# Gate and value products of chunks 1 to 5 by half-size Winograd products in PSUM lanes, the residual by accumulating transfers, and a new instruction order

## The chip, the cores and the metric

One core of a Trainium2 chip runs the whole program in one launch. The metric is device microseconds of one execution, less is better. Besides the timed runs there is one execution taken by the hardware profiler; its span goes from the first to the last instruction of the core. The engines are PE (TensorE, matmuls), ACT (ScalarE), DVE (VectorE), POOL (GpSimd) and SP (SyncE, which only issues transfers here).

## The reference

Inputs are q, k and v of shape (4 batches, 8 heads, 768 tokens, 64). Three heads (0, 2, 6) are causal; the five others see only the first 4 keys and the last 64.

```python
scores = q @ k.transpose(0, 1, 3, 2) / sqrt(64)          # masked, softmax, then @ v
x      = attention, heads side by side                   # 3072 tokens x 512
g      = x @ w_gate                                      # 512 x 1536
val    = x @ w_val                                       # 512 x 1536
ffn    = (0.5 * g * (1 + erf(g / sqrt(2))) * val) @ w_out    # 1536 x 512
out    = x + sigmoid(x @ w_res) * ffn                    # f32
```

## The kernel before

**Tiling.** The 3072 tokens are cut into six chunks of 512 (four tiles of 128): chunk 0 and 3 are the first four tiles of batches 0 and 2, chunks 1 and 4 are two tiles of one batch and two of the next, chunks 2 and 5 four tiles of batches 1 and 3. A chunk goes through attention (by pairs of heads: scores on PE, exp on ACT, masks on DVE, values on PE, normalizing on DVE into `xtok` in f32 and `x` in f16, transposes into `xT`), then gate and value, then the output product. Chunks overlap: while gate and value of one chunk run, the output product of the chunk before ends, and the next chunk's scores follow.

**Gate and value** (`gate_value`). There are 12 column tiles f of 128 for gate and for value. Each is four matmuls of 512 columns (the tokens; the weights are the stationary operand) into a PSUM bank. ACT makes the gelu (L1166), DVE multiplies with the value bank into `hT` (L1168). Chunk 0 starts in halves of 256 tokens (L1140, L1143).

**Output** (`output_fast`, all but half of chunk 0). The product h @ w_out is already done by Winograd's form of Strassen's scheme: tokens, inner dimension and columns are each halved, and seven products of half size replace eight. `sums` forms S1 to S4 from h (L1187), `weight_sums` T1 to T4 from w_out (L1204); two PSUM banks take the products, and partial results go out and are added by ACT and DVE (L1251, L1252, L1257). Then DVE multiplies by 1 + tanh (L1281) and adds x (L1286), and SP stores 256 KB per tile (L1292).

**Loads.** POOL issues the loads of q, k, v and of the weights, which convert f32 to f16 on the way (L577). Chunks 0 and 1 transpose q and k on PE (L709), the later ones by transposing transfers of SP (L754) into `qkt`; a further transfer copies one pair of heads of it to the lower partitions (`q`, L762).

**Order.** Every operation is a task with a duration, dependences, buffers and a priority. `Graph.schedule` plays the program through with fixed costs (`c_mm`, `c_act`, `c_dve`, and a cost per transfer) and writes a fixed sequence for every engine; `HINTS` replaces the priorities of single tasks by tuned numbers. Buffers come from pools, and a task waits for the last users of the slot that it gets. On the chip each engine then runs its sequence in order and waits on semaphores. In the first 20 us PE runs filler matmuls on a blank tile (L1333) where nothing else is ready; they end with the first gate product. From chunk 2 on many matmuls run as two halves of 64 columns (`mm`, L516 whole, L517 halves).

Of the kernel before, what the change touches and what calls it, by code (L numbers as in the profile page):

```python
# [43 lines left out]


HINTS = (
    "3:-58.9 11:-130.04 428:854.14 430:718.61 444:2782.08 457:-821.9 460:407.45 490:4205.68 521:1522.06 "
    "591:-818.43 610:-36.63 612:486.89 613:-2965.25 619:1544.03 621:-44.07 643:467.87 644:-881 646:4.3 656:119.6 "
    "664:25.04 673:629.62 675:-109.25 695:-2674.26 696:-1856.67 703:-881.5 706:-108.75 707:714.39 708:1939.7 "
    "711:270.02 712:497.18 716:476.22 720:652.56 738:638.32 743:520.23 744:3053.24 749:514.3 750:1799.28 "  # L50
    "751:2383.53 756:521.28 762:1469.72 764:4344.87 767:2237.74 787:-603.93 815:5053.25 817:2978.67 821:1231.87 "
    "824:1484.86 836:2402.62 837:798.1 841:706.04 848:-288.52 849:2997.07 876:2751.74 906:2555.54 913:1516.93 "
    "918:2437.99 919:1519.88 924:1537.25 931:1510.23 936:2384.32 949:2443.79 955:2089.28 967:2846.74 995:-227.38 "
    "1001:29.83 1002:3171.86 1003:3180.29 1004:1146.58 1007:2686.58 1012:1781.89 1040:-803.29 1043:1907.45 "
    "1045:1028.83 1046:667.33 1050:3229.28 1051:1536.45 1053:3573.03 1056:-1823.77 1084:4090.27 1110:2454.97 "
    "1111:2597.62 1117:2808.38 1123:2507.5 1128:2481.58 1129:2529.63 1134:2508.5 1146:2434.73 1152:2779.33 "
    "1153:3034.61 1158:3861.94 1165:2795.06 1171:3076.63 1176:2997.8 1185:5989.69 1188:2243.92 1189:2528.84 "
    "1192:2789.39 1193:2537.45 1194:3836.22 1208:3021.15 1215:6294.68 1263:3219.13 1268:5037.38 1283:4420.5 "
    "1308:4756.92 1311:3513.6 1317:3517.03 1321:3052.3 1329:5930.49 1330:3507.5 1335:3508.5 1336:3519.22 "
    "1341:4624.14 1345:3444.6 1353:3516.64 1354:3538.83 1357:2761.66 1365:3787.63 1366:5173.04 1372:5102.72 "  # L60
    "1386:5438.32 1392:4014.31 1393:4933.66 1418:5146.68 1430:4133.91 1441:5428.8 1452:5127.54 1457:2188.42 "
    "1462:4595.33 1464:5711.23 1467:9389.54 1468:4425.54 ~1471:550.69 1476:5611.77 1499:4504.13 1513:6742.83 "
    "1516:5340.27 1522:4510.5 1523:4585.63 1526:3632.38 1534:4503.02 1539:4253.34 1550:4463.64 1565:7711.51 "
    "1570:4506.5 1571:5085.34 1580:2427.42 1594:2466.44 1610:9272.71 1625:3048.93 1627:6036.71 1629:6167.81 "
    "1631:5064.12 1644:6476.5 1662:4125.72 1671:5044.95 1672:7314.6 1676:4967.2 1683:6427.71 1692:9540.12 "
    "1711:7387.16 1757:5137.62 1784:5507.1 1797:5469.41 1803:7562.23 1817:7773.49 1818:7478.69 1823:7672.83 "
    "1834:7419.08 1836:10250.4 1849:7490.55 "
# [123 lines left out]
VS_DMA = 0  # L191
LAT = {"pe": 0.20, "act": 0.10, "dve": 0.08, "pool": 0.12, "sp": 0.1}


class Graph:
# [205 lines left out]
    def emit(self):  # L401
# [31 lines left out]
        with nc.Block() as blk:  # L433
# [17 lines left out]
            @blk.sync  # L451
            def _(e):
                run("sp", e)
                for t in finals:
                    e.wait_ge(t.sem, 16)
# [6 lines left out]
def c_act(n):  # L462
    return 0.19 + n * 0.000834


def c_dve(n, rate=1.0, psum=True):
    return (0.125 if psum else 0.065) + n * 0.00104 / rate
# [6 lines left out]
def build_kernel(nc, q, k, v, w_gate, w_val, w_out, w_res, out):  # L474
# [17 lines left out]
    P_vs = Pool(many("vs", 2, [128, NT - 1, NHEAD, DHEAD + 1], FP16))  # L492
    P_vk = Pool(many("vk", 2, [128, 8, DHEAD + 1], FP16))
    P_qkt = Pool(many("qkt", 2, [128, 2, NPAIR, SEQ], FP16))
# [9 lines left out]
    P_hs = Pool(many("hS", 1, [128, 3, NF // 2, 2, 128], FP16))  # L504
    wt = sb("wt", [128, 4, NF // 2, 256], FP16)
    P_ga = Pool(many("gact", 4, [128, 512], FP16))
    P_sr = Pool(many("srs", 3, [128, 512], FP32))
# [5 lines left out]
    def mm(e, o, lhsT, rhs, **k):  # L513
# [8 lines left out]
        "gv": (4, one(6, 7, 5, 4, 3, 2)), "gv0": (4, one(6, 7, 5, 4)), "gvh": (4, one(7, 6, 4, 5)), "out": (2, one(6, 7)), "fin": (4, one(6, 7, 1, 0)), "warm": (1, one(7, 5)),  # L522
# [81 lines left out]
    def batch(b):  # L604
        if b not in batches:
            B_ = B()
            B_.v, B_.vs, B_.vk, B_.qkt = Buf(P_v), Buf(P_vs), Buf(P_vk), Buf(P_qkt)
            B_.vtok, B_.vstok, B_.qtok, B_.ktok = {}, {}, {}, {}

            B_.q6, B_.q6tok = None, {}  # L610
            batches[b] = B_
        return batches[b]

    def values(b, a, z, base, each, on_engines=False):
# [23 lines left out]
        if on_engines:  # L638
            ts = []
            for lo, hi, pr in ((1, 2, -75),) + (() if VS_DMA else ((2, 4, 130),)):  # L640
                for dst, src, off in ((0, 64, 1), (64, 0, 0)):
                    def vs(on, dst=dst, src=src, off=off, lo=lo, hi=hi):
                        def fn(e):
                            o = at(BB.vs)[dst:dst + 64, lo - 1:hi - 1, :, :].rearrange("p i h d -> p (i h d)")
                            i_ = at(BB.v)[src:src + 64, lo - off:hi - off, :, :].rearrange("p i h d -> p (i h d)")
                            return e.activation(out=o, in_=i_, func=AF.Copy) if on == "act" else e.tensor_copy(out=o, in_=i_)
                        return fn
                    n_ = (hi - lo) * 520
# [9 lines left out]
        for lo in cuts:  # L658
            hi = lo + 1 if each else z
            ts = []  # L660
            for dst, src, off in ((0, 64, 1), (64, 0, 0)):
                ts.append(G.add("sp", 1.2, (lambda lo=lo, hi=hi, dst=dst, src=src, off=off: lambda e: e.dma_start(
                    at(BB.vs)[dst:dst + 64, lo - 1:hi - 1, :, :].rearrange("p i h d -> p (i h d)"),
                    at(BB.v)[src:src + 64, lo - off:hi - off, :, :].rearrange("p i h d -> p (i h d)")))(),
# [7 lines left out]
    def loads_rows(c, si, b, a, z):  # L672
# [17 lines left out]
        for gi, (h0, h1) in enumerate(groups):  # L690
# [41 lines left out]
    def loads_natural(c, si, b, a, z):  # L732
# [33 lines left out]
        for i in range(a, z):  # L766
            BB.q6tok[0, i] = BB.q6tok[1, i] = t
# [677 lines left out]
```

The softmax here doesn't subtract the row's maximum and nothing guards it: scores larger than these inputs give would overflow.

## Time and profile before

| | |
|---|---|
| timed runs, us | 267.08, 266.18, 265.86; median 266.18 |
| span of the profiled execution, us | 263.7 |
| time of the profiled execution outside its span | not recorded |
| PE busy, us | 257.7 (98% of the span) |
| DVE, ACT, POOL busy, us | 181.6, 147.2, 89.3 |
| granted PE clock | 1.000 |
| first gate product starts, us | 19.7 |
| last matmul ends, us | 257.4 |
| transfers, MB (share of 16 engines) | POOL's queue 14.69 (67.5%), SP's queue 14.07 (28.0%) |

In the profile a row of a group has line, engine, operation, the tiles written and read, shapes and count, then busy time and the mean of one in ns, then idle time of the engine before it and who ended it. A row of the timeline has start, length, engine, line, operation and count. Lengths of matmuls overlap, so the rate is read from the starts.

### The profile page before, as it was taken

The numbers are of one execution on the slowest core, as the hardware profiler recorded it, in microseconds if no ns is written. First come the engines' busy times: TensorE is split into PE (matmuls) and PEld (weight loads), VectorE is DVE, ScalarE is ACT, GpSimd is POOL, SyncE is SP. The second block draws the span as 40 slices with busy tenths as digits, with TensorE's granted clock in tenths as the row PEclk, the third lists the DMA queues.
The fourth block names the chain that finished last, engine by engine and source line by source line (L and its number), as shares of the span: only waits on it lengthen the run. The fifth ranks groups of instructions, "written<-read, shape, count | busy, mean of one in ns | idle before, by whom it ended". The sixth has DMA issues, their size and how long they took to land.

```text
span 263.7 us, 7495 instructions
## 1 busy us (share of the span) xinstructions
PE 257.7 (98%) x3226; PEld 164.0 (62%) x3226; DVE 181.6 (69%) x378; ACT 147.2 (56%) x237; POOL 89.3 (34%) x127
## 2 busy tenths in 40 slices
PE   7999999999999999999999999999999999999993
PEld 6777655468444668544567444589655588655692
DVE  2698437798447888557898366888557689837655
ACT  2785467974244987423787242967243888233430
POOL 8999979506109973975000000000000000000003
PEclk9999999999999999999999999999999999999999
DMA  6999999999999999999996110004200004200003
GB/s 83 174 204 206 188 175 231 175 153 204 134 200 148 165 137 177 171 179 176 174 156 150 42 40 0 2 26 101 82 2 0 2 2 122 82 2 0 2 35 127
DMA packets 96513, 29.22 MB, mean 111 GB/s; under 512 B 84449, under 2 KB 93025, under 8 KB 96481
## 3 DMA queue, kind: packets, MB, share of 16 engines
q0 software_dynamic: 70320, 14.69, 67.5%
q1 hardware_dynamic: 26160, 14.07, 28.0%
q8 instruction: 25, 0.41, 0.7%
q14 instruction: 8, 0.06, 0.1%
HBM read 29.36 MB, written 6.29 MB: 135 GB/s over the span
## 4 chain that ended last, share of the span: by engine, by line
PE 95%; DMA 2%; DVE 1%; issue 0%; POOLq 0%
PE ps L516 50%; PE ps L517 32%; PE ps L893 5%; PE ps L1333 2%; PE ps L1017 2%; PE ps L709 2%; DMA qks<-in_q_dram 2%; PE ps L1106 2%; PE ps L984 1%; DVE otile L1281 1%; DVE otile L1286 1%; DVE otile L1257 0%; POOLq L1427 0%
## 5 line engine op out<-in xcount | busy, mean ns | idle before, releaser
L1166 ACT ACTIVATE gact<-ps 128x512 f16<-128x512 f32 x68 | 40.2, 597 | 73.5 <-PE ps L516 43.7
L1168 DVE SCALAR_TENSOR_TENSOR hT<-gact,ps 128x512 f16<-128x512 f16 x68 | 46.1, 686 | 48.0 <-PE ps L516 23.1
L516 PE MATMUL ps<-xT,wg 128*128 128x512 f16 (+1 forms) x208 | 50.0, 363 | 0.0
L516 PE MATMUL ps<-xT,wv 128*128 128x512 f16 (+1 forms) x202 | 49.0, 362 | 0.0
L1286 POOL TENSOR_TENSOR otile<-otile,xtok 128x256 f32<-128x256 f32 x3 | 2.4, 801 | 136.2 <-DVE otile L1281 136.2
L577 POOL DMA_DIRECT2D qks<-in_k_dram x36 | 28.0, 810 | 17.3 <-DMA qkt<-qks 13.9
L516 PEld LDWEIGHTS ps<-xT,wg 128*128 128x128 f16 x208 | 20.1, 98 | 20.0 <-DVE otile L1257 0.3
L516 PEld LDWEIGHTS ps<-xT,wv 128*128 128x128 f16 x202 | 19.4, 98 | 20.0 <-DVE hT L1168 0.5
L577 POOL DMA_DIRECT2D qks<-in_q_dram x36 | 28.4, 828 | 2.2 <-issue 1.4
L517 PE MATMUL ps<-xT,wv 128*64 128x512 f16 x204 | 28.3, 380 | 0.0
L577 POOL DMA_DIRECT2D va<-in_v_dram x24 | 21.3, 920 | 15.1 <-PE ps L516 15.1
L517 PE MATMUL ps<-xT,wg 128*64 128x512 f16 x192 | 26.3, 379 | 0.0
L909 ACT ACTIVATE ea<-ps 128x1024 f16<-128x1024 f32 (+2 forms) x24 | 21.1, 915 | 1.7 <-PE ps L893 1.6
L1257 DVE TENSOR_TENSOR otile<-otile,ps 128x256 f32<-128x256 f32 x33 | 13.6, 417 | 7.1 <-PE ps L517 4.7
L1226 ACT ACTIVATE srs<-ps 128x512 f32<-128x512 f32 x22 | 13.1, 595 | 9.1 <-PE ps L517 6.7
L517 PEld LDWEIGHTS ps<-xT,wv 128*64 128x64 f16 x204 | 11.5, 110 | 9.8 <-DVE hT L1168 0.3
L1084 DVE TENSOR_TENSOR xtok<-ps,rcp 128x512 f32<-128x512 f32 (+1 forms) x28 | 16.8, 606 | 0.2
L517 PEld LDWEIGHTS ps<-xT,wg 128*64 128x64 f16 x192 | 11.1, 110 | 9.0
L893 PE MATMUL ps<-qkt 64*128 64x64 f16 (+4 forms) x391 | 16.4, 213 | 0.0
L893 PEld LDWEIGHTS ps<-qkt 64*128 64x128 f16 x391 | 9.8, 94 | 8.0 <-issue 4.2
L516 PE MATMUL ps<-wo,hT 128*128 128x256 f16 (+1 forms) x84 | 14.4, 304 | 0.0
L1286 DVE TENSOR_TENSOR otile<-otile,xtok 128x512 f32<-128x512 f32 (+1 forms) x21 | 14.3, 691 | 0.2
(109 smaller groups left out, 437.4 us busy)
## 6 DMA issues: line engine op xcount, KB each, us to landing
out_dram<-otile SPq DMA_DIRECT2D x22, 256.0 KB, 2.4
va<-in_v_dram POOLq DMA_DIRECT2D x24, 128.0 KB, 17.6
qks<-in_k_dram POOLq DMA_DIRECT2D x32, 64.0 KB, 12.6
qks<-in_q_dram POOLq DMA_DIRECT2D x32, 64.0 KB, 13.0
wg<-in_moe_w_gate_dram POOLq DMA_DIRECT2D x3, 512.0 KB, 10.2
wv<-in_moe_w_val_dram POOLq DMA_DIRECT2D x3, 512.0 KB, 12.1
wo<-in_moe_w_out_dram POOLq DMA_DIRECT2D x4, 384.0 KB, 22.8
vs<-va SPq DMA_DIRECT2D x4, 260.0 KB, 7.9
```

The costliest lines, as they stand in the source:

```text
L516: return e.matmul(o, lhsT=lhsT, rhs=rhs, **k)
L517: return [e.matmul(o[h:h + 64], lhsT=lhsT[:, h:h + 64], rhs=rhs, **k) for h in (0, 64)][-1]
L577: return G.add(eng, issue, lambda e: e.dma_start(out_ap(), in_ap), deps, prio, bufs=bufs, dma=cost, name=name, grp=grp)
L709: return [e.transpose(out=at16(scr)[64 * x:64 * x + 64, (m * n + i) * 128:(m * n + i + 1) * 128], in_=piece(jj, h, i), identity=ident[:, : ...
L893: return [e.matmul(at(scr)[:, oo:oo + w], lhsT=side(BB, low, 1)[half, k0:k0 + 128], rhs=side(BB, low, 0)[half, qq:qq + w], start=True, sto ...
L909: return e.activation(out=o, in_=i_, func=AF.Exp, scale=SM_SCALE)
L1084: t2 = G.add("dve", c_dve(2 * n * 64), lambda e: e.tensor_tensor(out=xview(), in0=avv(0, DHEAD), in1=scale(), op=ALU.mult), [t1] + xdeps, ...
L1166: ta = G.add("act", c_act(512), (lambda gb=gb, ga=ga: lambda e: e.activation(out=at(ga)[:, :], in_=at(gb)[:, :], func=AF.Gelu))(), [tg], p ...
L1168: th = G.add("dve", c_dve(512), (lambda vb=vb, ga=ga, f=f: lambda e: e.scalar_tensor_tensor(out=hv(f), in0=at(ga)[:, :], scalar=0.5, in1=a ...
L1226: tas.append(G.add("act", c_act(512), (lambda rb=rb, sr=sr: lambda e: e.activation(out=at(sr)[:, :], in_=at(rb)[:, :], func=AF.Tanh, scale ...
L1257: return G.add("dve", c_dve(256), lambda e: e.tensor_tensor(out=dst(), in0=dst(), in1=at(D)[:, 0:256], op=ALU.add), [t, k], pr, bufs=[D, o ...
L1286: fn = (lambda ot=ot, lt=lt, w=w: lambda e: e.tensor_tensor(out=at(ot)[:, w], in0=at(ot)[:, w], in1=at(xbuf)[:, lt, w], op=ALU.add))()
```

## The change

From chunk 1 on (the second), f = 6 to 11 of gate and of value are computed by Winograd's scheme too. The column tiles are paired as (6, 9), (7, 10), (8, 11), the 512 inner rows and the 512 tokens are halved. For each pair, and for gate and value each, a chain of seven products of 128 x 128 x 256 (two matmuls each, as the inner half is 256) runs in a lane of two PSUM banks, with four areas AL, AR, BL, BR. There are three lanes, which first take the plain products of f = 0, 1, 2.

- `gv_sums` makes T1 to T4 of both weights once, on DVE (T3 in place of the weight).
- `fast` makes S1 to S4 of `xT` per chunk on DVE, then per chain: products 1 and 5; ACT copies AL to BL (`seed`); ACT or DVE copies AR to an output tile (`hold`); product 6 onto BL; DVE adds BL and the held part to AR (`merge`); product 7 onto BL, products 2 and 3 onto AL and AR; a second merge into BR; product 4 onto BL. Gelu and the multiplication read two halves in two banks.
- The residual: for all tiles but those of chunk 0 and the last two, `store_x` writes x to the output with one transfer of SP per chunk, and the gated product is added in DRAM by an accumulating transfer of POOL. The add on DVE falls away there.
- The first loads of q and k (heads 0 to 3 of chunk 0) come as f32 by SP into an `xtok` buffer and are converted by ACT or DVE.
- `qkt` is split into K by batch (`kT`, 2 buffers) and Q by chunk (`qT`, 2 buffers of 512 tokens); `vs` is narrower, `hS` smaller with a second part in `wS`, `srs` has 2 buffers in place of 3, `wt` 3 parts in place of 4.
- `c_act` and `c_dve` get other constants, two order constraints change, and `HINTS` is replaced as a whole, so that the order of all engines is new. SP then has, in chunk 1 and 2's time, transposes of batch 3's first tiles ahead of those of chunk 3.

```diff
 HINTS = (
-...
+...
 )
 def c_act(n):
-    return 0.19 + n * 0.000834
+    return 0.17 + n * 0.000834
 def c_dve(n, rate=1.0, psum=True):
-    return (0.125 if psum else 0.065) + n * 0.00104 / rate
+    return 0.15 + n * 0.00105 / (2.0 if rate > 1.0 else 1.0)
...
-    P_qkt = Pool(many("qkt", 2, [128, 2, NPAIR, SEQ], FP16))
+    P_kt = Pool(many("kT", 2, [128, NPAIR, SEQ], FP16))
+    P_qt = Pool(many("qT", 2, [128, NPAIR, 512], FP16))
...
+        "lane": (LANES, [(4, 5), (2, 3), (0, 1)]),
+        "gv": (4, one(6, 7, 5, 4, 3, 2, 1, 0)), ...
...
+            for m in range(2):                          # loads_rows, chunk 0
+                for j, src in ((1, k), (0, q)):
...
+                    t = G.add("sp", 0.65, (lambda dst=dst, src=src, m=m: lambda e: e.dma_start(
+                        dst(), src[b, m:m + 3:2, lo:hi, :].rearrange("h (p j) d -> p h (j d)", j=n)))(), [], ...
+                    t = G.flex({"dve": (c_dve(512, 1.0, False), cast("dve")), "act": (c_act(512), cast("act"))}, [t], ...
...
+            if c and f >= FA:                           # gate_value
+                break
+            laned = c > 0 and f < LANES
...
+    def gv_sums():
...
+            t1 = add(wt_[:, 0], blk(0, 1), blk(0, 0), here, 0)
+            t2 = add(wt_[:, 1], blk(1, 1), wt_[:, 0], [t1] + here, 1)
+            t4 = add(wt_[:, 2], blk(1, 0), wt_[:, 1], [t2] + here, 2)
+            t3 = add(blk(0, 1), blk(1, 1), blk(0, 1), [t1] + here + gv_tail, 3)
+    def fast(c, xtbuf, xttoks, h, toks, hv, lanes_):
...
+        s1 = add(lambda: S(0), lambda: A(1, 0), lambda: A(1, 1), ALU.add, xd, [xs, xtbuf])
+        s2 = add(lambda: S(1), lambda: S(0), lambda: A(0, 0), ALU.subtract, [s1] + xd, [xs, xtbuf])
+        s3 = add(lambda: xs3[:, :, :], lambda: A(0, 0), lambda: A(1, 0), ALU.subtract, xd + xs3_last, [xtbuf])
+        s4 = add(lambda: S(2), lambda: A(0, 1), lambda: S(1), ALU.subtract, [s2] + xd, [xs, xtbuf])
...
+        for q in range(2 * NP):
...
+            es = Buf(P_ot)
...
+            def merge(o, deps, ps=ps, es=es):
+                return G.add("dve", c_dve(256), lambda e: e.tensor_tensor(out=at(ps)[:, o], in0=at(ps)[:, BL],
+                             in1=at(es)[:, 0:256], op=ALU.add), deps, p_, bufs=[ps, es], name="merge")
+            t15 = product([("A11", "B11", AL, True), ("S1", "T1", AR, False)], list(free))
+            seed = copy((lambda ps=ps: at(ps)[:, BL]), (lambda ps=ps: at(ps)[:, AL]), [t15], [ps], "seed")
+            hold = copy((lambda es=es: at(es)[:, 0:256]), (lambda ps=ps: at(ps)[:, AR]), [seed], [ps, es], "hold")
+            t6 = product([("S2", "T2", BL, False)], [seed])
+            m1 = merge(AR, [t6, hold])
+            t7 = product([("S3", "T3", BL, False)], [m1])
+            t23 = product([("A12", "B21", AL, False), ("S4", "B22", AR, False)], [m1])
+            m2 = merge(BR, [t7])
+            t4 = product([("A22", "T4", BL, False)], [m2])
...
+    def store_x(c, xbuf, xtoks):
+        n = 2 if c == len(CHUNKS) - 1 else 4
+        r0 = c * 512
+        stored[c] = G.add("sp", 0.65, lambda e: e.dma_start(
+            out[r0:r0 + n * 128, :].rearrange("(i p) d -> p i d", p=128), at(xbuf)[:, 0:n, :]), ...
...
+            if c >= ACCUM and not end:                  # output_fast
+                t = G.add("pool", 1.0, (lambda ot=ot, r0=r0: lambda e: e.dma_start(out[r0:r0 + 128, :], at(ot)[:, :],
+                          accum_op=ALU.add))(), ends + [stored[c]], pr - 3000, bufs=[ot], dma=1.0, name="out")
+                t.late = 0.5
+                continue
...
-            t.order += ph(c, "sc") + (ph(c, "xT") if f > 1 else [])
+            t.order += ph(c, "sc") + (ph(c, "xT") if f > 1 else []) + (ph(c - 1, "fw") if LANES <= f < FA else [])
...
-            t.order += [x for f, x in gv if f == NF - 2] + ph(c, "xT")
+            t.order += [x for f, x in gv if f == (FB - 1 if c else NF - 2)] + ph(c, "xT")
```

## Prediction

> **What bounds the kernel now.** I read the shares of the engines first, then the chain that ended last, then a table of stages, then single rows for durations.
>
> ```profile
> PE 257.7 (98%) x3226; PEld 164.0 (62%) x3226; DVE 181.6 (69%) x378; ACT 147.2 (56%) x237; POOL 89.3 (34%) x127
> PE 95%; DMA 2%; DVE 1%; issue 0%; POOLq 0%
> ```
>
> TensorE is busy 98% of the span and makes 95% of the chain. So the span is the number of matmul columns plus a head and a tail; the other engines matter only where PE waits for them. The next table has, for four stretches, the length and the busy time (instructions) of PE, of weight loads, of DVE, ACT and POOL, the clock, the DMA share and GB/s: gate and value of chunk 1, attention of chunk 2, then the same two one chunk later.
>
> ```profile
> 63.70:84.80 21.10, 21.10 (x110) 9.94 (x110) 13.06 (x22) 7.20 (x13) 8.54 (x12) 1.00 1.61 171
> 84.80:105.30 20.50, 20.47 (x300) 14.30 (x300) 17.27 (x41) 17.45 (x25) 14.82 (x21) 1.00 2.04 156
> 105.30:128.10 22.80, 22.80 (x113) 10.70 (x113) 13.45 (x24) 8.17 (x15) 14.99 (x20) 1.00 1.87 174
> 128.10:143.90 15.80, 15.80 (x247) 11.35 (x247) 14.05 (x34) 13.72 (x21) 0.00 (x0) 1.00 1.24 170
> ```
>
> PE never idles here; DVE has 60% in gate and value but 85 to 90% in attention, and DMA is loaded until about 128 us. The rates of PE come from neighbouring rows of the timeline (start, length, count):
>
> ```profile
> 63.50 0.82 PE L516 MATMUL ps<-wt,hT 128*128 128x256 f16 x6
> 64.15 0.82 PE L516 MATMUL ps<-wo,hT 128*128 128x256 f16 x6
> 64.81 1.03 PE L516 MATMUL ps<-xT,wg 128*128 128x512 f16 x4
> ...
> 82.07 1.46 PE L516 MATMUL ps<-xT,wv 128*128 128x512 f16 x6
> 83.37 1.03 PE L516 MATMUL ps<-xT,wg 128*128 128x512 f16 x4
> ```
>
> Start to start, twelve 256-column matmuls take 1.31 us (0.109 each) and six of 512 columns 1.30 us (0.2165). Half-width matmuls cost exactly half: their weight loads are hidden. From 185 us on, each is a pair of 64-column halves, and such a pair takes the same time.
>
> **What the skill says.** The Trainium skill, "TensorE: Matmul & The Clock Gate", section "Wait — 56ns, not 53.3ns?", gives N / 2.4 GHz plus about 2.5 ns; that is 0.216 and 0.109 us, as the rows have it. "VectorE: DVE Perf Modes", section "The perf-mode tier table (the rule you actually need)", lets `tensor_tensor` run at double rate only with 16-bit SBUF operands and at single rate with PSUM: the trace has 0.42 us both for 512 f16 columns and for 256 f32 columns with PSUM. "PSUM — Partial Sum Buffer", section "PSUM bank collisions raise a hardware error", says that two engines must not be in a bank at once, which is why a lane's products and merges take turns; no run here shows a collision. "DMA: Bandwidth & Descriptors", section "SWDGE vs HWDGE vs iDMA", lets only GpSimd accumulate in a transfer, so the new outputs join its one queue, the one that q0 of the page shows at 67.5%.
>
> **The matmuls.** Per chunk from 1 to 5, f = 6 to 11 of gate and of value were 48 matmuls of 512 columns: 48 x 0.2165 = 10.4 us. Now 6 chains of 14 half matmuls: 84 x 0.109 = 9.2 us. Saved 1.24 a chunk, 6.2 us in five. Counting the whole program gives the same: 240 of 512 columns less, 420 of 256 more. Everything else on PE stays.
>
> **The head.** The profile's chain begins
>
> ```profile
> 1.32 4.32 DMA qks<-in_q_dram
> 5.64 0.04 issue
> 5.68 0.64 PE ps L709 x16
> ```
>
> so the first transposes wait for a converting load from GpSimd. Now SP loads f32 (an unloaded 256 KB transfer of SP lands in 2.4 us), ACT converts in 0.6 us: first transposes near 0.9 + 2.4 + 0.6 + 0.2 = 4.1 instead of 5.7. GpSimd issues two loads fewer (1.66 us) ahead of V and the weights. Up to the first gate product the changed order also has 7 cold filler matmuls less (3.93 us for 41: 0.096 each) and 13 warm ones less (0.065 each): 1.5 us. I take -1.5, ends -2.5 and 0.
>
> **What the chains cost DVE and ACT.** New on DVE: 60 merges x 0.417 (the row of L1257; the output is now PSUM, which no row shows: 0.3 to 0.5, I keep 0.417) = 25.0; 20 sums of x x 0.42 = 8.4; 7 holds x 0.42 = 3; 8 weight sums of 768 columns x 0.55 = 4.4. Gone: 18 residual adds x 0.684 = 12.3, 6 copies of output partials 2.5, small ones 2. Sum +24, DVE near 206 us, 80% of the new span. ACT: 30 seeds and 23 holds x 0.38 = 20, 6 more partials 2.3, four conversions 2.4: +25, 66%. All of it lies beside PE as long as it is in time. In gate and value of chunk 1, DVE goes from 13.06 to 13.06 + 5.0 + 1.7 + 0.6 - 1.4 = 19.0 us in 19.9: 95%; one chunk later 19.3 in 21.6. That cover is thin, so I price waits. A chain is 0.44 + 0.38 + 0.22 + 0.42 + 0.22 + 0.42 + 0.22 + gelu 0.60 = 2.9 us and seven handovers, some 4 us, twice per lane: 8 us. The order puts the chains of chunk 2 into 84 x 0.109 + 24 x 0.2165 = 14.4 us of PE work over three lanes, so only the last steps lie bare: 0.3 us a chunk, +1.5 (0.025 per merge; ends 0 and 0.2).
>
> **The transfers.** The residual (18 adds, 4 to 5 MB written twice) leaves DVE for one x store per chunk on SP and 18 accumulating stores behind GpSimd's loads. Every `hold` takes an output tile that such a store must have left. From chunk 2's outputs on, no load is left in that queue, and I put no wait. For chunk 1's they queue among loads:
>
> ```profile
> out_dram<-otile SPq DMA_DIRECT2D x22, 256.0 KB, 2.4
> qks<-in_k_dram POOLq DMA_DIRECT2D x32, 64.0 KB, 12.6
> ```
>
> In the loaded stretch SP's own outputs took 6.5 to 8.5 us. The first holds of chunk 2 come some 5 us into its gate stage, about 108 us, the second store is issued near 99: 0 to 5 us late, I take 0 and leave it to a rival. Behind a late hold on ACT stand the gelus that free the lanes.
>
> Second, the copy of Q and K of one pair to the lower partitions (L762) for chunk 2:
>
> ```profile
> 80.98 0.67 SPq L762 DMA_DIRECT2D q<-qkt  x1
> ...
> 90.03 0.38 PE L893 MATMUL ps<-q 64*128 64x384 f16 x2
> ```
>
> Such copies took 7.6 us, so it landed at 88.6 with 1.4 us to spare. Chunk 2's scores now come 1.5 + 1.24 = 2.7 us sooner, with the same 5.3 us of PE work from the first score to this use: wanted at 87.3. The transposes ahead of the copy wait for loads and each other, not for PE. So PE waits 1.3 us (0 to 4: an x store and four transposes of batch 3 are put ahead of it). In the new order chunk 3's K transposes wait for chunk 2's scores, because batch 3 took the other K buffer early: from 93.5, ten transposes of 1.5 to 1.8 us and an x store that waits for the last norm end near 113, landing 8 us later at 121 for a use at 124: spare 3 us, no cost.
>
> **Sum.** 263.7 - 6.2 - 1.5 + 1.5 + 1.3 = 258.8 us of span. The tail of 6.3 us after the last matmul (merge, gate, add, store) keeps its instructions. The median of the runs shown, 266.2, is 2.5 above the span; the profiled run's time outside the span isn't given, so I carry 2.5 over: 261.3 us.
>
> **Rivals.**
> (1) All waits hidden: the chains have cover and the transfers come in time, and the head gains up to 2.5. For it: PE idled nowhere in 238 us. Against: DVE at 95% of a stage. 257.5 to 258.5.
> (2) The transfers between 80 and 125 us take the gain: the holds wait 4 us for the accumulating stores and the copy 3 us, 5.7 more than above: 267, no difference to measure. For it: landings of 8 to 13 us in that queue. Against: it touches chunk 2 only.
> (3) Slower: DVE in order becomes the bound. The place is the merge on which two products wait; the price is 60 times what PE does not cover. The saving is 7.7 us, less 1.3 for the copy, and the bound of a change that can be told is 0.5% (1.3 us, about what this measurement resolves): with 7.7 / 60 = 0.13 us bare per merge, a third of a merge's 0.42, it is slower. At 0.2 us: 263.7 - 7.7 + 12 + 1.3 + 2.5 = 272. For it: attention already has DVE at 85 to 90%, so lateness isn't recovered there. Against: three lanes, and plain products to fill.
> That the change doesn't do what it says I exclude: the matmuls are counted.
>
> **Chances.** Forecast 0.47 (259 to 263), rival 1 0.14, mixtures and rival 2 between 263 and 267.5 0.21, rival 3 0.18. Of the middle case about half lies below 264.85. Faster 0.71, same 0.11, slower 0.18. Range 257 to 268; the forecast's own is 259 to 264.
>
> **What would show it.** Right: half-width products at 0.109 us, gate and value stages of some 20 us, first transposes near 4 us, the same tail. Wrong: idle time of PE at the products charged to DVE's merges (rival 3), to ACT's holds behind an output's landing, or to the copy's landing near 87 us (rival 2); a first gate product still near 19.7 us would take the head's share.

## The result and the profile after

The changed kernel takes 277.1 us (median of four runs, 273.9 to 280.5), the kernel before 266.0 us (265.6 to 267.1): a ratio of 1.0335, with a 95% interval from 1.0272 to 1.0398. I had predicted 261.3 us and a range from 257 to 268. The profiled execution has a span of 274.3 us against 263.7. The changed kernel's runs lie 6.6 us apart and those of before 1.4; the ratios, here and below, leave out runs more than 1.5% above the fastest of their kernel, so a ratio can lie below that of the two medians. A part of this spread is seen in the traces: a stretch at half clock near the start is longer in some executions than in others.

The shares of the engines, the row of the granted clock and the chain by engine, from the page of the changed kernel:

```profile
PE 256.1 (93%) x3452; PEld 181.6 (66%) x3452; DVE 201.2 (73%) x445; ACT 170.4 (62%) x304; POOL 104.2 (38%) x143
PEclk9569999999999999999999999999999999999997
PE 74%; DMA 11%; DVE 6%; POOL 2%; ACT 2%; issue 1%; SPq 0%; POOLq 0%; DVEq 0%
```

TensorE made 95% of the chain before and makes 74% now. What took its place is DMA with 11% and DVE with 6%, and the second and third slices, from 7 to 20 us, were mostly at half clock. DVE's and ACT's totals came out near the forecast (206 and 172 us).

To see where the time went I cut the span at two events, the first gate product and the last matmul. For every matmul in the timeline I took its start less the start of the one before plus that one's columns at 0.42 ns each: what is left over is a gap in which TensorE had nothing to run.

| us, profiled executions | before | after |
|---|---|---|
| start to the first gate product | 19.7 | 25.9 |
| from there to the start of the last matmul | 239.5 | 239.9 |
| of it, matmuls | 230.8 | 225.0 |
| of it, gaps of 15 to 115 ns | 8.3 | 8.2 |
| of it, gaps over 115 ns | 0.4 | 6.6 |
| last matmul to the end | 4.4 | 8.6 |

So there are three losses of about the same size, a head of +6.1, waits of +6.2 and a tail of +4.2 us, and one gain of 5.8 us, the one that was meant. They add up to +10.7, the difference of the spans. The short gaps are mostly the changes between matmuls of different shape (64 and 128 rows, or 64 and 128 columns of weights), about 95 ns each and some 80 of them in both kernels.

**The head.** First the longest piece that the chain has at the start, then the timeline of TensorE (start, length, count, and in brackets the idle time and what ended it), then two stretches of the table by stage, whose last columns are clock, DMA share and GB/s; behind them rows and a stretch of the kernel before:

```profile
1.82 7.25 DMA xtok<-in_k_dram
```

```profile
5.53 0.64 PE L768 MATMUL ps<-ident,qks 128*64 128x128 f16 x16 [0.85 <-POOL ident L565]
9.77 0.64 PE L768 MATMUL ps<-ident,qks 128*64 128x128 f16 x8 [3.61 <-ACT qks L741]
10.34 1.03 PE L1522 MATMUL ps<-blank 128*128 128x128 f16 x8
```

```profile
0.00:6.00 6.00, 4.08 (x50) 3.92 (x50) 1.39 (x7) 2.75 (x4) 4.80 (x11) 1.00 0.69 141
6.00:18.00 12.00, 8.39 (x111) 5.43 (x105) 5.07 (x11) 5.99 (x11) 9.29 (x20) 0.57 1.59 199
```

```profile
5.68 0.64 PE L709 MATMUL ps<-ident,qks 128*64 128x128 f16 x16 [0.69 <-DMA qks<-in_q_dram]
6.25 0.84 PE L1333 MATMUL ps<-blank 128*128 128x128 f16 x12
7.02 0.64 PE L709 MATMUL ps<-ident,qks 128*64 128x128 f16 x16
```

```profile
6.00:16.00 10.00, 9.98 (x213) 7.60 (x207) 7.53 (x21) 7.69 (x15) 9.86 (x20) 1.00 1.74 183
```

The second K load of SP, issued at 1.82 us, landed at 9.07. TensorE had sixteen transposes at 5.5 us and then nothing for 3.6 us. The record of the clock falls to one half at 7.7 us, within this wait, and rises again at 18.0: a row of eight filler matmuls took 1.03 us, where before a row of twelve took 0.84. The first transposes did not wait for their loads, which had landed at 3.6 and 4.3 us, but for the identity mask, which the new order puts behind four loads of GpSimd.

**The waits.** Part of the chain in chunk 2's gate and value stage, in order of time:

```profile
109.20 5.26 POOL va L607 x6
114.46 0.05 issue
114.51 16.49 DMA out_dram<-otile
131.00 0.02 issue
131.03 0.39 ACT otile L1306
...
131.51 0.43 DVE ps L1310
```

This is a `hold` behind an accumulating store. The store was issued at 114.5 us, behind six loads of V on GpSimd, and took 16.5 us to land; the hold on ScalarE waited for it, the merge for the hold, and a product of TensorE for the merge, 1.2 us. The other long gaps: 0.6 us at later merges of the same chunk and the next; 2.5 us in all where a chunk passes from its lanes to its output products, 0.1 to 0.8 us in each chunk; 1.1 us at 229 us for which the profile names no releaser; 0.5 us for a transfer that transposes the normed x at 155 us; 0.4 us in chunk 0, and two of 0.1. The passage of chunk 1 is seen on DVE, and the product that waits for its sum on TensorE:

```profile
93.83 0.69 DVE L1358 TENSOR_TENSOR hS<-hS,hT 128x1024 f16<-128x1024 f16 x1
94.43 0.42 DVE L1358 TENSOR_TENSOR wS<-wS,hT 128x512 f16<-128x512 f16 x1
```

```profile
94.92 0.27 PE L545 MATMUL ps<-wt,hS 128*128 128x256 f16 x1 [0.53 <-DVE wS L1358]
```

From 88 us on DVE has hardly a pause: merges, the lanes' last gate products (L1335), and then the sums of h (L1358), most of which wait for the lanes' last results. At the other passages the profile names ScalarE more often than DVE: a score product waits for an exponential (0.4 us in chunk 2, 0.3 in chunk 3), an output product for a partial result that ScalarE carries out (0.4 us in chunk 4).

**The tail.** The last pieces of the chain, after:

```profile
265.14 0.70 DVE otile L1463
...
266.38 0.88 POOL out_dram L1467
267.26 0.87 POOLq L458
```

and of before, which is followed by one store of SP that lands at 263.7:

```profile
260.34 0.02 issue
260.37 0.77 DVE otile L1286
```

The last two output tiles in the new order are those of the last chunk's first pair, and they leave by two accumulating stores that GpSimd issues one after the other; the second lands some 7 us after its issue begins.

### The profile page after: what moved, and what is told of

Same layout as the page of the kernel before. It is cut to its first block, busy times and chain, and to the rows that moved or that the text cites. A ratio compares the mean times of both kernels' runs of the same rounds, so it can differ in the third digit from the quotient of the medians.

```text
span 274.3 us, 8120 instructions
## 1 busy us (share of the span) xinstructions
PE 256.1 (93%) x3452; PEld 181.6 (66%) x3452; DVE 201.2 (73%) x445; ACT 170.4 (62%) x304; POOL 104.2 (38%) x143
## 4 chain that ended last, share of the span: by engine, by line
PE 74%; DMA 11%; DVE 6%; POOL 2%; ACT 2%; issue 1%; SPq 0%; POOLq 0%; DVEq 0%
PE ps L545 33%; PE ps L546 29%; DMA out_dram<-otile 6%; PE ps L957 5%; DMA xtok<-in_k_dram 3%; DMA xT<-x 2%; PE ps L1522 2%; PE ps L768 2%; POOL va L607 2%; PE ps L1081 2%; DVE hT L1335 1%; PE ps L1170 1%; DVE hS L1358 1%; DVE wS L1358 1%; DVE hT L1358 1%
## 5 line engine op out<-in xcount | busy, mean ns | idle before, releaser
L1467 POOL DMA_DIRECT2D out_dram<-otile x18 | 16.2, 929 | 92.0 <-DVE eb L1009 51.8
L1236 ACT ACTIVATE gact<-ps 128x512 f16<-128x512 f32 x38 | 22.6, 598 | 30.8 <-PE ps L545 19.7
L545 PE MATMUL ps<-xT,wv 128*128 128x512 f16 (+1 forms) x172 | 38.4, 337 | 0.2 <-DVE hT L1208 0.2
L545 PE MATMUL ps<-xT,wg 128*128 128x512 f16 (+1 forms) x172 | 37.6, 337 | 0.4 <-DMA xT<-x 0.4
L607 POOL DMA_DIRECT2D qks<-in_q_dram x35 | 29.2, 911 | 17.4 <-DMA kT<-qks 10.6
L1310 DVE TENSOR_TENSOR ps<-ps,otile 128x256 f32<-128x256 f32 x60 | 24.8, 430 | 10.8 <-PE ps L545 5.0
L607 POOL DMA_DIRECT2D va<-in_v_dram x24 | 21.4, 908 | 11.4 <-PE ps L1170 10.4
L545 PEld LDWEIGHTS ps<-xT,wg 128*128 128x128 f16 x172 | 16.4, 98 | 12.4 <-DMA xT<-x 0.9
L545 PEld LDWEIGHTS ps<-xT,wv 128*128 128x128 f16 x172 | 16.5, 98 | 10.9 <-issue 0.5
L1335 DVE SCALAR_TENSOR_TENSOR hT<-gact,ps 128x512 f16<-128x512 f16 x30 | 19.7, 683 | 4.5 <-PE ps L546 2.4
L1306 ACT ACTIVATE ps<-ps 128x256 f32<-128x256 f32 x30 | 11.1, 370 | 12.8 <-PE ps L545 7.4
L545 PE MATMUL ps<-wo,hT 128*128 128x256 f16 (+1 forms) x114 | 18.9, 296 | 0.0
L546 PE MATMUL ps<-xT,wg 128*64 128x512 f16 (+1 forms) x144 | 18.2, 344 | 0.0
L546 PE MATMUL ps<-xT,wv 128*64 128x512 f16 (+1 forms) x144 | 17.9, 344 | 0.0
L957 PE MATMUL ps<-qT,kT 64*128 64x64 f16 (+4 forms) x391 | 17.1, 217 | 0.4 <-ACT ek L1055 0.2
## 6 DMA issues: line engine op xcount, KB each, us to landing
wg<-in_moe_w_gate_dram POOLq DMA_DIRECT2D x3, 512.0 KB, 10.2
```

Of the source, the lines that this page charges most:

```text
L545: return e.matmul(o, lhsT=lhsT, rhs=rhs, **k)
L546: return [e.matmul(o[h:h + 64], lhsT=lhsT[:, h:h + 64], rhs=rhs, **k) for h in (0, 64)][-1]
L607: return G.add(eng, issue, lambda e: e.dma_start(out_ap(), in_ap), deps, prio, bufs=bufs, dma=cost, name=name, grp=grp)
L957: return [e.matmul(at(scr)[:, oo:oo + w], lhsT=side(BB, qb, low, 1)[half, k0:k0 + 128], rhs=side(BB, qb, low, 0)[half, qq:qq + w], start=T ...
L1236: ta = G.add("act", c_act(512), (lambda gb=gb, ga=ga, gw=gw: lambda e: e.activation(out=at(ga)[:, :], in_=at(gb)[:, gw], func=AF.Gelu))(), ...
L1310: return G.add("dve", c_dve(256), lambda e: e.tensor_tensor(out=at(ps)[:, o], in0=at(ps)[:, BL], in1=at(es)[:, 0:256], op=ALU.add), deps, ...
```

## The experiments

All but one of the kernels below are the changed kernel with an edit made on the finished order, before the waits are worked out from it, so that nothing moves but what the edit names. `move` puts a task at a place in an engine's order, `drop` takes one out. The theory at the start was H: the head is the largest part, by K's lateness and then the clock. The rival was L: the lanes' merges and DVE are what costs.

**The f32 first loads undone.** The two first loads of Q and K go back to GpSimd:

```
  ld.fn = lambda e: e.dma_start(dst, src[0, 0:4, 0:512, :]...)   # f16 destination, converting
  G.move(ld, "pool", 0)
  for t in (the other f32 load, both casts): G.drop(t, [ld])
  G.move(t_ident, "pool", 2)
```

> The changed kernel with its f32 first loads undone: the first Q and K come by two converting loads of GpSimd, as before, with the identity mask right behind them; every other engine's order is kept. Theory H (the head is the larger part of the loss: K landed at 9.1 us, TensorE idled 3.6 us and then ran at half clock until about 18 us): first K transposes before 8 us, no stretch at clock 0.50, first gate product at 19.5 to 21 us instead of 25.9, and the time 7 to 10 us under the changed kernel's 277.1: 267 to 270. Rival L (the lanes and their merges are what costs; an earlier start is only given back later): the first gate product comes as early, but the end moves by less than 3 us: 274 to 277.

Measured: 276.1 us (271.0 to 279.4), first gate product at 26.7. Neither theory had this. The first transposes come at 5.7 us, but the order of the changed kernel has no fillers between them, TensorE waits 1.3, 1.1 and 0.4 us up to 10.1 us, and in the profiled execution the clock is at one half from 7.6 to 24.7 us. One part alone could not be judged as long as the clock goes with it.

**The clock alone.** 55 filler matmuls into the wait for K.

```
  w = Task("pe", 0.06, filler, [], 1e9, name="warm"); pe.insert(behind the first transposes, w)   # 55 times
```

> The changed kernel with 55 more filler matmuls between the first transposes and the ones that wait for K, so that TensorE is busy through the wait. It parts the wait for K from the half clock after it. If the half clock is a cost of its own: K's transposes still start at 9.5 to 10 us, the clock stays at 1.00 from 8 to 18 us, first gate product at 21.5 to 23 us, the time 3 to 5 us under the changed kernel: 272 to 274, and the runs lie closer together than 273.9 to 280.5. If only the data are late and the clock costs nothing: within 1 us of 277.1.

Measured: 275.9 us (273.6 to 277.9), ratio 1.0357 (1.0309 to 1.0405). The first gate product came at 24.5. The 55 fillers took 5.2 us, since the first 39 of them still ran at half clock, 0.107 us apart where the others took 0.056, so that K's transposes were put off from 9.8 to 11.3: I had overfilled by 1.5 us. (In this execution the record of the clock has no entry before 10.4 us, and the views print 1.00 where there is none.) The fitted number is in a run below.

What the half clock costs is better read from five profiled executions with the same order up to the first gate product: the changed kernel and the runs below on the hold, the tail, the merges and the accumulating transfers. From the start of K's second transposes to the first gate product they take 14.3, 15.1, 15.3, 16.1 and 16.8 us, and full clock comes at 12.4, 14.7, 15.6, 18.0 and 19.4 us, in the same order: some 0.36 us for each us of half clock.

**The hold without the store.** The sixth lane's hold of chunk 2 into an idle buffer.

```
  es.pool, es.slot = (an idle x16 buffer), 0
  hold.deps = [d for d in hold.deps if d is not the store] + before
```

> The changed kernel with one hold of chunk 2 (the sixth lane's) put into an idle buffer, so that it does not wait for the accumulating store that was issued at 114.5 us and landed at 131.0. If this wait is bare: ScalarE's 2.5 us wait at 128.6 us and TensorE's waits of 1.05 and 0.27 us at 132.0 and 133.4 us go, the handover waits behind them (137.4, 139.7) shrink, and the time falls by 1.5 to 2.5 us, to 274.6 to 275.6. If DVE's queue is the limit there anyway: less than 0.7 us.

Measured: 274.4 us (271.4 to 277.4), ratio 1.0292 (1.0228 to 1.0357); in the profile 0.26 and 0.43 us of gap at the two products, where it was 1.2 and 0.4. This is not the test that was meant: the edit took the wait from the hold and left it on the hold's two merges, where it is bare only if the store is later still. It was in a later run of this kind (the one with the copies ahead on SP's queue), whose DVE reads

```profile
129.64 0.43 DVE L1352 TENSOR_TENSOR ps<-ps,x 128x256 f32<-128x256 f32 x1 [3.42 <-DMA out_dram<-otile]
```

with 3.0 us of gap on TensorE. So where the wait was in place it cost between nothing (the run with the tail alone) and 3.0 us. In the two executions in which it was longest, this one and that of the 55 fillers (2.9 us), the record then shows half clock for 3.41 us.

**The tail alone.** The last chunk's first pair with a residual add on DVE and plain stores.

```
  a = Task("dve", ..., tensor_tensor(ot, ot, xtok, add)); insert(behind the last "gated" of the tile)
  G.move(t, "sp", end); t.fn = plain dma_start
  G.drop(x store of the last chunk)
```

> The changed kernel with the last chunk's first pair of output tiles stored as before: DVE adds the residual (two adds of 512 columns more), SP stores plainly, and the x store of that chunk is left out. If the accumulating stores are what makes the tail long: from the last matmul to the end 4.5 to 5.5 us instead of 8.4, the time 3 to 4 us less: 273 to 274. If two more adds on DVE take it back: less than 1 us.

Measured: 270.5 us (267.6 to 273.9), ratio 1.0103 (1.0066 to 1.0139). From the last matmul to the end 4.8 us, as expected, 3.8 less. The medians lie 6.6 us apart, more than the 3 to 4 expected; the rest is not explained by this edit, and the start varies from execution to execution. The end of its chain (two adds on DVE at L1628, and then SP):

```profile
268.27 0.68 DVE otile L1505 x2
268.95 0.02 issue
268.97 0.69 DVE otile L1628
```

The long tail was a cost of the accumulating stores, and DVE's two adds, 1.4 us, don't take it back.

**Why K landed late.** GpSimd's loads wait until the f32 loads are converted.

```
  G.move(t_ident, "pool", 0)
  first GpSimd load.deps += the four casts
```

> The changed kernel with GpSimd's loads held back until the four f32 loads have been converted; the identity mask comes first. It asks why K landed at 9.1 us. If GpSimd's loads share the transfer engines with it: all four f32 loads land by 5.5 us (K's first by 4.5) and K's transposes start before 6 us instead of at 9.8; the held loads land some 4 us later, so the first gate product is not earlier than 22 us and the time not under 273. If SP's loads are that slow by themselves: K still lands at 8 us or later.

Measured: 280.5 us (279.6 to 281.5), ratio 1.0552 (1.0505 to 1.0600). Time from issue to landing of the four f32 loads (smallest, median, largest), first with GpSimd's loads beside them, in the changed kernel, then without:

```profile
DMA to landing us min/median/max: 2.8/5.1/8.3
```

```profile
DMA to landing us min/median/max: 2.7/3.5/4.2
```

K's transposes came at 5.0 and 6.5 us. The loads were late because they shared the transfer engines. The Trainium skill, "DMA: Bandwidth & Descriptors", section "Queues, rings and completion order", says that each transfer engine takes turns between the queues that have work for it; 8.3 us beside GpSimd's queue and 4.2 us without it agree with that. GpSimd's loads of Q and K, held back, then made TensorE wait 3.9 us, the clock was at one half from 10.6 to 27.7 us, and the first gate product came at 29.8: here the one set of loads is early only at the price of the other.

**More work on DVE at the merges.** An unused operation of 256 columns before each merge.

```
  merge: lambda e: [e.tensor_tensor(out=es[:, 256:512], in0=es[:, 0:256], in1=es[:, 0:256], op=max),
                    e.tensor_tensor(out=ps[o], in0=ps[BL], in1=es[:, 0:256], op=add)]
```

> The changed kernel with an extra DVE operation of 256 columns (some 0.42 us, its result unused) ahead of each of the 60 merges: 25 us more on DVE, at the place that the third rival names. If the merges are bare (DVE in order is the bound there): nearly all of it shows, 15 to 25 us more. If three lanes and plain products cover them: 2 to 8 us more. Near nothing would say that DVE has slack even here.

Measured: 280.4 us (279.1 to 285.7), ratio 1.0532 (1.0500 to 1.0563): over the changed kernel 3.3 us by the medians, 5.2 by the ratios. The groups of the page, the merge and the added operation:

```profile
L1354 DVE TENSOR_TENSOR ps<-ps,otile 128x256 f32<-128x256 f32 x60 | 25.7, 428 | 0.0
L1353 DVE TENSOR_TENSOR otile<-otile 128x256 f32<-128x256 f32 x60 | 25.3, 421 | 4.3 <-PE ps L588 2.1 <-PE ps L587 1.4
```

TensorE's gaps over 115 ns go from 6.6 to 12.0 us. So of 25.3 us more on DVE at that very place 5.4 came out as gaps, 0.09 us for each merge. The merges are covered, though not deeply. Bare merges on DVE are not what made the kernel slower.

**Tail, clock and the hold's buffer at once**, with 38 fillers, fitted to the wait.

> The changed kernel with the idle buffer for the hold, the last chunk's plain residual and 38 fillers (fitted to the 3.6 us wait for K) at once. If the three losses are separate: tail 4.8 us, no bare wait over 0.5 us at the merges, first gate product at 22.5 to 23.5 us, time 266 to 269. If another wait takes their place in the middle: 270 or more.

Measured: 268.9 us (268.2 to 269.4), ratio 1.0112 (1.0087 to 1.0137). First gate product at 23.6, tail 4.8, no gap over 0.2 us at a merge; the runs now lie 1.2 us apart. The fillers themselves ran at half clock, 0.11 us each; the record's first entry, full clock, is at 10.2 us, when K's transposes start:

```profile
6.11 4.21 PE L1564 MATMUL ps<-blank 128*128 128x128 f16 x38
10.25 0.64 PE L810 MATMUL ps<-ident,qks 128*64 128x128 f16 x16
10.82 0.62 PE L1564 MATMUL ps<-blank 128*128 128x128 f16 x8
```

A new wait stands in the middle, in the timeline of TensorE:

```profile
97.56 0.39 PE L999 MATMUL ps<-qT,kT 64*128 64x512 f16 x1 [1.34 <-DMA q<-qT]
```

That is the copy of Q and K of chunk 2 to the lower partitions, which the prediction had priced at 1.3 us. In the changed kernel itself it cost 0.14.

**All accumulating transfers undone**: the edit of the tail for all 18 output tiles, and no x stores.

> The changed kernel with its accumulating transfers undone: DVE adds the residual to each of the 18 output tiles (12.3 us more on DVE), SP stores plainly, the x stores are left out; the lanes, the f32 loads and the order stay. If the accumulating transfers are behind the waits of TensorE over 0.1 us in the middle (6.3 us more than before): these fall to 3.5 us or less, the tail to some 5 us, and the time by 5 to 7 us, to 270 to 272. If the lanes' work on DVE is behind them: they stay or grow, and only the tail's 3 to 4 us come back, or less.

Measured: 271.6 us (270.7 to 274.3), ratio 1.0250 (1.0188 to 1.0312). The tail is 4.8 us, the gaps over 115 ns are 6.6 us as in the changed kernel, but they are other ones: no hold, copy or transposed x is waited for any more, and attention products and merges wait for DVE in their place. So the accumulating transfers are behind the waits for transfers, and in these two profiles what they cost there is as much as they spare DVE.

**The loads again, with the clock kept up**: the first experiment, 34 fillers in the first waits, and the edits of the tail and the hold.

> The first experiment again, but with its clock kept up: the f32 first loads undone, 34 fillers set into the waits of the first transposes (8, 8 and 18), and the hold's idle buffer and the last chunk's plain residual as in the run with all three. Theory: the half clock hid what the loads themselves cost. Then the second halves of Q and K are used near 10 us at full clock, the first gate product comes at 21 to 22.5 us, and the time is 266 to 268. If the f32 loads are no loss with the clock held: the first gate product stays at 23 to 24 us and the time at 268 to 270.

Measured: 268.8 us (267.2 to 270.4), ratio 1.0126 (1.0083 to 1.0169). The first gate product comes at 21.5, as expected, 2.1 us before the run with f32 loads and fillers. The time is no better: TensorE now waits 2.5 us for the copy of Q and K.

**The copies ahead on SP's queue.** On top of the run before:

```
  for t in (the two copies of chunk 2): G.move(t, "sp", behind the first x store)
```

> The same, and on SP's queue the two copies of Q and K of chunk 2 to the lower partitions put ahead of a transpose and a copy of the batch after, which wait for later loads. If the copy is late because of what stands ahead of it in the queue: TensorE's wait of 1.5 us at the scores near 97 us goes, and the time falls by 1 to 1.5 us against the run before, to 264.5 to 267, level with the kernel before. If it is late by its own inputs: no change.

Measured: 267.7 us (265.1 to 273.0, 22 runs, nine of them over 270), ratio 1.0026 (1.0008 to 1.0044). The first copies go out at 84.1 us instead of 89 and the wait for them is gone. This ratio is the best of all, level with the kernel before within 0.1 to 0.4%, and not faster.

**All repairs at once**, now with the merges freed of the store too, and 50 fillers.

```
  for u in (the hold and its two merges): u.deps = [d for d in u.deps if d is not the store] + before
```

> All repairs at once: f32 first loads undone, 50 fillers in the first transposes' waits (12, 12 and 26), the copies of Q and K of chunk 2 ahead on SP's queue, the last chunk's plain residual, and the hold of chunk 2 in the idle buffer with its two merges freed of the store as well (in the earlier runs with that buffer the wait for the store had only gone over from the hold to its merge on DVE, where it cost 3.0 us in the run with the copies ahead). If head, tail and these two waits are what stood between the change and its gain: first gate product at 21 to 22 us, no wait over 0.7 us behind it, some 237.5 us from there to the last matmul, 263 to 265.5. If the lanes bring a loss of their own that other waits had hidden: 266 or more.

Measured: 270.7 us (266.6 to 273.0), ratio 1.0065 (1.0036 to 1.0093). First gate product at 21.7, no wait for a hold, none for the copy. In their place TensorE waits 2.3 us at 151.7 for the transposed x of chunk 3, whose transfer SP issued at 143.9 between those of the next batch. From the first gate product to the last matmul it is 240.1 us, where 237.5 had been expected.

**The same hold edit with the f32 loads.**

> The run with fillers, plain last residual and the hold's buffer, f32 loads kept, now with the hold's merges freed of the store as well. If that wait was bare in part of the runs there: 0 to 2 us under its 268.9, and never a wait for an output's landing at the merges. If the store had always landed by then: 268.5 to 269.5.

Measured: 269.9 us (267.8 to 271.6), ratio 1.0168 (1.0132 to 1.0204). No merge waited for a store, but the time is not under that of the run that it was to better. With four runs of each and a head that varies, it says nothing on the worth of this wait.

**The kernel before with the f32 loads alone**: four loads of SP and four conversions on ScalarE for its two first loads.

```
  drop(loads 390, 391 of GpSimd)
  SP: ld32 q, k, q, k first;   ACT: cast q, k, q, k behind the table load
```

> The kernel before with one part of the change alone: its first Q and K loads become four f32 loads of SP with conversions on ScalarE; nothing else moves, fillers included. If the f32 loads cost by themselves (they share the transfer engines with GpSimd's next loads, which now start 1.7 us earlier): K's first transposes at 8 to 10 us instead of 7.0, first gate product at 20.5 to 23 us, 1 to 4 us slower, 267 to 270. If they gain as forecast, 1.5 us: first transposes near 4.1 us and 264 to 265. If the second halves of Q and K, near 9.7 us in both, set the head: 265.5 to 266.5.

Measured: 270.0 us (268.0 to 270.2), ratio 1.0133 (1.0093 to 1.0172). The timeline of TensorE at the start, then the table by stage:

```profile
5.39 0.41 PE L751 MATMUL ps<-ident,qks 128*64 128x128 f16 x8
7.29 0.41 PE L751 MATMUL ps<-ident,qks 128*64 128x128 f16 x8 [1.48 <-ACT qks L1451]
7.64 0.84 PE L1375 MATMUL ps<-blank 128*128 128x128 f16 x12
9.41 1.06 PE L751 MATMUL ps<-ident,qks 128*64 128x128 f16 x16 [0.94 <-ACT qkt L765]
10.41 1.25 PE L1375 MATMUL ps<-blank 128*128 128x128 f16 x10
```

```profile
6.00:16.00 10.00, 7.78 (x108) 6.16 (x110) 3.07 (x6) 4.78 (x8) 9.21 (x18) 0.66 1.68 195
```

Two waits of 1.5 and 0.9 us, and behind the twelve fillers of 0.84 us come ten of 1.25: half clock, by the record from 8.6 to 15.4 us. The first gate product comes at 24.6 instead of 19.7, everything behind it is as before. This part of the change is a loss by itself, of some 4 us, and it takes the clock along although every filler is still there.

**The lanes and the order alone**: f32 loads and accumulating transfers undone, 50 fillers.

> Of the change the lanes and the order alone: the f32 loads undone with 50 fillers in the first waits, and all accumulating transfers undone (DVE adds the residual, SP stores plainly, no x stores). If the accumulating transfers and x stores are what makes copies and transposes of chunks 2 and 3 late: no wait of TensorE over 0.7 us behind the head, first gate product at 21 to 22 us, and 264 to 266.5. If DVE with the residual back on it (213 us busy) is then the limit: waits of 0.3 to 0.7 us at attention products and merges, 6 us or more in all, and 266.5 to 269.

Measured: 267.9 us (267.7 to 268.3), ratio 1.0078 (1.0064 to 1.0093). First gate product at 21.6. From there to the last matmul 239.8 us, as in the kernel before, with 7.0 us of gaps over 115 ns. The largest waits of its matmuls (total, times, longest), those of the head left out:

```profile
PE ps L1123 <- issue: 0.6, 2, 0.4
PE ps L587 <- DVE wS L1400: 0.5, 1, 0.5
PE ps L587 <- DVE ps L1352: 0.5, 1, 0.5
...
PE ps L587 <- DVE xtok L1190: 0.3, 1, 0.3
```

No single one is large: the sums of h, a merge, normed rows, each a few tenths where DVE is a little late, some where ScalarE is, and two without a releaser. DVE is busy 212 us. Even without its companions, the lanes' saving of 5.8 us is spent in this order.

## Why the prediction was wrong

**The matmuls, -6.2.** Right: -5.8 us of matmul time between the first gate product and the last matmul, in the changed kernel and, within 0.1 us, in the runs with the tail and the clock repaired.

**The head, -1.5.** Wrong in sign, and the largest error: +6.1. The failing step is "an unloaded 256 KB transfer of SP lands in 2.4 us", taken for all four loads. The first two landed in 2.8 and 2.9 us, the last two, issued at 1.8 and 2.3 us, in 7.3 and 8.3. They were not unloaded. I had counted GpSimd's next loads, which start 1.7 us sooner, as a gain; they are what shares the engines with the f32 loads (at most 4.2 us without them, 8.3 with them). The early pair gained nothing either, because the first transposes, forecast for 4.1 us, waited until 5.5 for the identity mask, which the sum leaves out. The second failing step counted 20 fillers less as time saved, at 0.096 and 0.065 each. In the kernel before they fill the waits, so that leaving them out saves nothing, and the clock, which the sum leaves out too, fell in the wait for K. The Trainium skill, "TensorE: Matmul & The Clock Gate", section "What's actually happening", says that an idle window of about 3.4 us puts the array back to half clock; the traces show the fall after less. In the changed kernel it came at 7.7 us, 1.6 us into the wait of 3.6, and in the kernel before with f32 loads after a wait of 1.5 us, as the one of 0.9 began. Waits of 2.5 us in the middle of two runs (the loads again, all repairs at once) left it at 1.00, so the length of one wait does not decide. The parts: with the old loads and fillers the new order's first gate product is at 21.5 us, 1.7 after that of before; f32 loads with full clock from 10.2 us make it 23.6, 2.1 more; the longer half clock makes it 25.9, 2.3 more in this execution.

**The merges, +1.5.** Of the right size. The products' gaps at the lanes' merges and copies in the changed kernel are 1.8 us over 60 merges, 1.2 of it the one behind the store. Rival 3 put the turning point at 0.13 us bare for each merge. It was 0.03, and 0.09 more with twice the work. The outcome was on this rival's side, its mechanism was not what happened. What the step left out is the passage from a chunk's lanes to its output products, 2.5 us over five chunks: the lanes' last results come at the end of the stage, and other work queues behind them. The profile names the sums of h on DVE for 0.7 us of it in chunk 1 and for up to 0.4 in chunk 2, and mostly ScalarE's exponentials and partial results for the rest; no experiment parts the two. I had costed the last steps of a chain at 0.3 us a chunk but not what is queued behind them.

**The copy of Q and K, +1.3.** It was 0.1 us in the changed kernel, and 1.5 to 2.5 us in the three runs that repaired the head, the tail and the hold but left the copies in their old place. The term and its place were right. Its size does not follow the head alone, as I had it: 1.8 us in the run with the tail alone, whose first gate product came at 26.1, and 0.3 in that with the hold alone, at 23.4.

**The hold, 0, left to rival 2.** The mechanism of rival 2 is in the chain word for word, an accumulating store behind loads in GpSimd's queue, but at the sixth lane and not at the first, and with a landing of 16.5 us (13.5 to 19.4 in the other executions) where I had taken 8 to 13. It cost 1.2 us in the profiled execution and up to 3.0 in others.

**The tail, "keeps its instructions".** Wrong: +4.2 us. I had read it off the last pair's outputs, which did keep theirs. The new order puts the first pair's outputs last, and those end in accumulating stores. I had that order at hand and did not follow its last two stores to the end. The 6.3 us that I gave as the time after the last matmul was that after the last matmul on the chain; the last matmul of all starts at 259.2, so the tail of before is 4.4. The 257.4 us in the table of the kernel before is that earlier one, too.

**Not priced at all**: 0.5 us for the transposed x of chunk 3, and 1.1 us near 229 us for which the profile names no releaser. Stalls at which TensorE had nothing to wait for come again in most other profiles of the changed order, at 0.2 to 1.8 us and near the same few matmuls (the one of 229 us in seven executions). All of them end 1.2 to 1.5 us after a packet of 16 KB on the queue that the page calls "instruction" (q8), here 228.08 and 229.47 us. That TensorE had run out of fetched instructions would fit; no run tests it.

In the sum: predicted span 258.8, measured 274.3, 15.5 more: 7.6 at the head, 4.2 at the tail, 3.4 in waits (6.2 against 1.5 + 1.3), 0.4 in matmuls.

What the runs show beyond that: with tail, head and copies repaired the time comes down to that of before and not below it. Each repaired wait for a transfer brought up the next, from the hold to the copy to the transposed x, and taking the transfers away brought up DVE. In the kernel before, all of this had stood hidden behind matmuls: its gaps over 115 ns are 0.4 us. That some other order could keep part of the 5.8 us is not excluded; no run here does.

## What to carry to other kernels

A saving on the engine that is busy 98% of the time uncovers what its matmuls had been hiding. Before counting it, list what becomes due earlier (copies, transposes, sums on the next engine) with its spare time, and expect the next one to show when the first is repaired. At the start of a program a filler matmul between two waits need not be waste: here 3.6 us without one were followed by ten at half clock, and the run with fitted fillers was 2.3 us earlier at the first gate product. And follow the last store of the new order to its landing: a transfer that accumulates through GpSimd at the end cost 4 us that an add on DVE and a plain store do not.

## What was not expected of the hardware

A wait of 1.5 us and the beginning of a second, with eight transposes and twelve fillers between, were followed by half clock for 6.8 us. In all sixteen traces every stretch of the clock's record that the end of the trace does not cut is a whole multiple of 3.41 us: at half clock 3.41, 6.83, 10.24 and 17.07. How many of them it will be changes between executions of the same order at the start (one to three, or no full clock at all up to 19.4 us), and what decides that is not shown. The runs of the changed kernel lie 6.6 us apart; two kernels with the same 38 fillers had 1.2 and 3.8, so fillers alone don't settle it.

The record has no entry before full clock is first granted, between 3.7 and 19.4 us, and the views print 1.00 there. The spacing of the fillers shows half clock up to that time in every trace: 0.107 us for 128 columns, and 0.056 after it.

The last of SP's four loads of 256 KB took 8.3 us beside what GpSimd had put in its own queue, and 4.2 us without it. An accumulating store of 256 KB landed after 5.0 us (median), 7 us at the very end, and 13.5 to 19.4 us behind six loads of V; SP's plain stores of the same size took 2.4 us (median) in the kernel before.
